# The first weight transfer of a decode kernel, as two transfers of 64 partitions

## The chip, the cores and the metric

The kernel runs on one core of a Trainium2 chip. A core has five engines that run side by side and meet only at semaphores: TensorE (PE; its weight loads are shown as PEld), VectorE (DVE), ScalarE (ACT), GpSimd (POOL) and SyncE (SP). Data is brought from the chip's memory (HBM) into the core's own memory of 128 partitions by sixteen DMA engines. In this kernel every transfer is issued by SP, whose instructions appear in the profile as SPq.

The metric is the device time of one execution in microseconds. The kernel before was run three times: 364.06, 364.42 and 364.50, median 364.42.

## The reference

The kernel computes one decode step for 8 sequences: a gated sum of attention over a window of a key/value cache and a small multilayer network.

```
x = A_x                                       # 8 x 1 x 576, bf16
g = sigmoid((x * gate_w).sum(-1))
q = (x @ wq)                                  # wq: 576 x 4096; 32 heads of 128
k, v = last W = 2048 rows of the caches       # 16 KV heads, each for two query heads
p = softmax(q . k * 128 ** -0.5)
a = (p @ v) @ wo                              # wo: 4096 x 576
h = gelu(layernorm(x) @ w1 + b1)              # w1: 576 x 4608
b = h @ w2 + b2                               # w2: 4608 x 576
out = g * a + (1 - g) * b
```

Each of the two caches contributes 8 sequences x 16 heads x 2048 rows x 128 values in bf16, 67 MB. With the weights some 154 MB have to be read for an output of 9 KB.

## The kernel before

All operations are first described to a planner (`_Plan`, lines 39 to 164), not issued. `add` describes one operation on one engine with its dependencies and an estimated cost; `dma` (line 56) describes a transfer with the issuing engine, a semaphore and a size. A transfer may also have `after`, other transfers that must be issued earlier on the queue without being waited for. `schedule` (line 62) goes through all operations by their estimated times and so fixes the order on every engine. It models one shared stream for transfers of at least 65,536 bytes and charges each issue 0.35 us of the engine's own time (lines 98 to 103). `emit` (line 141) then writes each engine's instructions in this order, with the semaphore waits that the dependencies need. A wait on a DMA semaphore is a wait for a count: each transfer adds 16 when it has landed, so an operation that needs two transfers on one semaphore waits for 32, one that needs three for 48.

The core's memory is one arena. Its largest part, `RAW`, has four slots of 32 KB in each partition and some room behind them. At the start the slots hold weights: the main part of the query matrix (rows 0 to 511, `wq_m`, 32 KB in each partition) lies in slot 0, `w1` in slot 3, and the last 64 rows of the query matrix (`wq_r`, lines 357 and 358) behind `w1`. These 64 rows of 4096 values are cut in two, so that they fill 128 partitions with 2048 values (4 KB) each: partition 2k has the first half of row 512 + k, partition 2k + 1 the second. `xT` is laid out to match: the matmuls over this part (`q_fn`, lines 506 to 515, t = 4) contract over all 128 partitions with weights of x that are zero in every other one.

Lines 407 to 418 describe the first transfers, all on SP and chained by `after` in this order: `d_wqr` (the last rows of the query matrix, 512 KB), `d_wqm` (its main part, 4096 KB), x (9 KB), the gate's weights, two biases, `d_w1m` and `d_w1r` (4608 and 576 KB). The list `dwq` holds the two query transfers; the query matmuls `q_pe` depend on both and on the transposed x.

Behind them SP issues the stream (lines 586 to 594): 16 transfers of K and 16 of V, 4096 KB each, alternating from the second K on (`load_item`, line 613, issue at line 618), then parts of `w2` (line 865) and `wo` (line 836), and at the end the output (line 903). The first two K go into slots 1 and 2, which are free from the start. Every later transfer waits on SP until its slot is free: K slots are freed by the DVE transposes (line 718), V slots by the matmuls with the softmax weights (lines 755 and 188), slot 0, for the first V, by `q_pe`, and slot 3, for the third K, by the matmuls over `w1`.

For each K item the DVE transposes the keys, PE computes the scores (line 732 and the held matmuls of line 175), DVE takes the maximum (line 645), ACT the exponential (line 649), and DVE and ACT spread the result (lines 668 and 674) for the matmuls with V. The query itself is made once, from 13.9 to 25 us: x is transposed, multiplied with the query weights, rearranged and copied (lines 422 to 537). At the very end the last three parts of `w2` are multiplied in (line 579), the sum is copied out (lines 900 and 901) and stored.

Of the kernel before, what the change touches and what calls it, by code (L numbers as in the profile page):

```python
# [38 lines left out]
class _Plan:  # L39
# [16 lines left out]
    def dma(self, eng, fn, semkey, nbytes, deps=(), name=None, after=(), prio=0):  # L56
        op = _Op(eng, fn, deps, name, self.DMA_ISSUE, after=after, is_dma=True, dma_sem=semkey, nbytes=nbytes, prio=prio)
        op.idx = len(self.all)
        self.all.append(op)
        return op  # L60
# [134 lines left out]
def build_kernel(nc, A_x, A_k_cache, A_v_cache, A_wq, A_wo, B_x, B_w1, B_b1, B_w2, B_b2, gate_w, out):  # L195
# [29 lines left out]
    with ExitStack() as es:  # L225
# [129 lines left out]
        wq_m = RAW[:, 0:4 * 4096].rearrange("p (t c) -> p t c", t=4)  # L355
        W1O = (ND - 1) * DE
        WQR = W1O + 4 * F + F // 2
        wq_r = RAW[:, WQR:WQR + 2048]
# [21 lines left out]
        add, dma = P.add, P.dma  # L380
# [23 lines left out]
        o_on8 = add("pool", lambda e: e.memset(ones8, 1.0), name="ones8", cost=0.15)  # L404


        d_wqr = dma("sp", lambda e: e.dma_start(wq_r, A_wq[512:576, :].rearrange("k (s c) -> (k s) c", s=2)), "wq", 64 * 8192, name="d_wqr")
        d_wqm = dma("sp", lambda e: e.dma_start(wq_m.rearrange("p t c -> p (t c)"), A_wq[0:512, :].rearrange("(p t) c -> p (t c)", t=4)), "wq", 512 * 8192, name="d_wqm", after=[d_wqr])
        dwq = [d_wqm, d_wqr]
        d_x = dma("sp", lambda e: e.dma_start(x_sb, x2), "x", 8 * D * 2, name="d_x", after=[d_wqm])  # L410
        d_gw = dma("sp", lambda e: e.dma_start(gw_sb, gate_w.partition_broadcast(1)), "g", D * 2, name="d_gw", after=[d_x])
        d_b1 = dma("sp", lambda e: e.dma_start(b1c, B_b1.rearrange("(c f) -> c f", c=FC)), "b", F * 2, name="d_b1", after=[d_gw])
# [500 lines left out]
def bass_gated_mix__sliding_block_cached__mixer_channel_mlp__decode_kernel(  # L913
    nc: bass.Bass,
    A_x: bass.AP,
    A_k_cache: bass.AP,
    A_v_cache: bass.AP,
    A_wq: bass.AP,
    A_wo: bass.AP,
    B_x: bass.AP,  # L920
    B_w1: bass.AP,
    B_b1: bass.AP,
    B_w2: bass.AP,
    B_b2: bass.AP,
    gate_w: bass.AP,
    out: bass.AP,
):
    build_kernel(nc, A_x, A_k_cache, A_v_cache, A_wq, A_wo, B_x, B_w1, B_b1, B_w2, B_b2, gate_w, out)
# [28 lines left out]
```

## Time and profile before

| | before |
|---|---|
| three runs, median | 364.42 us |
| the profiled execution's own time | 364.27 us |
| its span, first to last instruction | 363.0 us |
| mean granted TensorE clock | 0.958 |
| packets of the data queue | 6092, 154.30 MB |
| read from HBM over the span | 425 GB/s |
| first issue on SP | 0.80 us |
| first landing that an engine waits for (x) | 13.86 us |
| last issue on SP (the output) | 361.61 us |

The span is counted from the first instruction to the last; the profiled execution's own time has 1.3 us more around it. The profile's page lists each engine's busy time, then the span in 40 slices of 9.1 us: each digit is a tenth of a slice. The row "GB/s" is what the DMA engines moved in each slice. Its table of queues has the data transfers as q1; q8 and q14 fetch instructions. "The chain that ended last" goes back from the last instruction, at each step to what released it. Other views used below are the list of DMA issues (KB of each, median us from issue to landing), the chain in order of time (start, duration, what), the timeline of one engine (start, duration, engine, line, operation) and the view by windows: for stretches of the span the busy time and number of instructions of each engine, the granted clock, the DMA share and GB/s. In that last view a DMA packet is counted whole in the stretch in which it starts, so that the share of a short stretch can be over 1.

### The profile page before, as it was taken

Reading aid. Unit: us, or ns where it says so; the run is one execution under the profiler, and the core shown is the slowest. Engines: PE = TensorE matmul, PEld = TensorE weight load, DVE = VectorE, ACT = ScalarE, POOL = GpSimd, SP = SyncE. Lnnn points to the kernel's source line nnn. Section 1 sums busy time; section 2 is a strip of 40 time slices with the busy share of each in tenths; the row PEclk is TensorE's granted clock in tenths of the full one; section 3 lists DMA queues with packets and bytes.
Section 4 is the critical chain, followed back from the end, with each engine's and each line's share of the span. In section 5 each row is a group of like instructions: output and inputs, shape, how many; then the busy total and the mean of one; then the engine's idle time right before and its main releaser. Section 6 shows DMA issues by size and latency. Waiting matters only on the chain.

```text
span 363.0 us, 4821 instructions
## 1 busy us (share of the span) xinstructions
PE 297.9 (82%) x1954; PEld 125.3 (35%) x1423; DVE 231.4 (64%) x166; ACT 168.6 (46%) x130; POOL 22.9 (6%) x52
## 2 busy tenths in 40 slices
PE   0456366999999979998897979997989698999875
PEld 0111000434252615242433417150615152436742
DVE  0452989576666694929385768566675949295720
ACT  1022106656647463663637373838374554656000
POOL 9032030000010000000100000000000000003000
PEclk9976598999999998999999989999999999999999
DMA  8999999999999999999999999999999999999996
GB/s 347 436 437 406 455 412 455 412 455 412 450 415 451 415 451 413 441 426 441 426 441 426 435 430 437 430 437 428 437 430 437 430 435 430 437 430 433 415 430 257
DMA packets 6102, 154.45 MB, mean 426 GB/s; under 512 B 694, under 2 KB 840, under 8 KB 1228
## 3 DMA queue, kind: packets, MB, share of 16 engines
q1 hardware_dynamic: 6092, 154.30, 98.8%
q8 instruction: 8, 0.13, 0.1%
q14 instruction: 2, 0.02, 0.0%
HBM read 154.29 MB, written 0.01 MB: 425 GB/s over the span
## 4 chain that ended last, share of the span: by engine, by line
DMA 56%; DVE 27%; PE 14%; issue 1%; ACT 1%; SPq 0%; POOL 0%
DMA arena<-in_A_k_cache_dram 47%; DVE arena L718 21%; PE ps L175 6%; DMA arena<-in_B_w_dram 6%; DMA arena<-in_A_x_dram 3%; DVE arena L668 2%; PE ps L188 2%; PE ps L755 2%; PE ps L732 2%; DVE arena L645 1%; PE ps L501 0%; PE ps L579 0%; DVE arena L557 0%; DVE arena L521 0%; ACT arena L536 0%
## 5 line engine op out<-in xcount | busy, mean ns | idle before, releaser
L718 DVE STREAM_TRANSPOSE arena<-arena 128x4096 f32<-128x4096 f32 (+1 forms) x34 | 141.7, 4175 | 21.9 <-DMA arena<-in_A_k_cache_dram 21.9
L674 ACT ACTIVATE arena<-arena 32x2048 bf16<-32x2048 bf16 x60 | 114.5, 1908 | 71.4 <-DVE arena L668 42.9
L175 PE MATMUL ps<-arena 128*128 128x512 bf16 (+3 forms) x531 | 136.1, 402 | 0.0
L188 PE MATMUL ps<-arena 128*128 x840 | 109.5, 277 | 7.3 <-issue 1.2
L188 PEld LDWEIGHTS ps<-arena 128*128 x840 | 81.4, 97 | 34.3 <-issue 19.0
L732 PE MATMUL ps<-arena 128*128 128x512 bf16 x128 | 51.4, 401 | 27.6 <-DVE arena L718 26.1
L645 DVE TENSOR_REDUCE arena<-ps 128x1 f32<-128x2048 f32 x16 | 36.7, 2291 | 53.8 <-PE ps L175 53.8
L732 PEld LDWEIGHTS ps<-arena 128*128 128x128 bf16 x128 | 12.5, 98 | 131.7 <-issue 75.3
L649 ACT ACTIVATE arena<-ps,arena 128x2048 bf16<-128x2048 f32 x16 | 40.7, 2543 | 0.5
L646 ACT ACTIVATE arena<-arena 128x1 f32<-128x1 f32 x16 | 3.2, 203 | 63.5 <-DVE arena L645 63.5
L755 PE MATMUL ps<-arena 128*128 128x256 bf16 x184 | 25.3, 272 | 1.1 <-DVE arena L663 1.1
L755 PEld LDWEIGHTS ps<-arena 128*128 128x128 bf16 x184 | 16.9, 99 | 18.8 <-issue 14.6
L668 DVE STREAM_TRANSPOSE arena<-arena 128x1024 f32<-128x1024 f32 x15 | 18.1, 1205 | 2.9 <-ACT arena L649 2.9
L579 PE MATMUL ps<-arena 128*8 128x288 bf16 (+1 forms) x140 | 9.6, 286 | 4.0 <-DMA arena<-in_A_wo_dram 3.3
L739 POOL MEMSET arena<- 128x4096 f32 x1 | 3.5, 3511 | 148.2 <-PE ps L175 148.2
L685 PE MATMUL ps<-arena 128*128 128x512 bf16 x16 | 6.5, 407 | 6.5 <-ACT arena L649 5.2
L629 POOL COPY arena<-arena 32x64 bf16<-32x64 bf16 x16 | 3.7, 229 | 123.3 <-PE ps L175 122.4
L901 ACT ACTIVATE arena<-ps 8x288 bf16<-8x288 f32 x1 | 0.4, 402 | 19.5 <-PE ps L579 19.5
L422 DVE COPY arena<-arena 8x128 bf16<-8x128 bf16 x2 | 0.5, 228 | 13.9 <-DMA arena<-in_A_x_dram 13.9
L579 PEld LDWEIGHTS ps<-arena 128*8 128x8 bf16 (+1 forms) x140 | 5.8, 86 | 9.9 <-DMA arena<-in_A_wo_dram 3.3
L900 DVE CAST arena<-ps 8x288 bf16<-8x288 f32 x1 | 0.4, 446 | 12.3 <-PE ps L579 12.3
L557 DVE TENSOR_TENSOR arena<-arena 128x1152 f32<-128x1152 f32 x1 | 1.4, 1358 | 9.7 <-ACT arena L555 9.7
(106 smaller groups left out, 94.0 us busy)
## 6 DMA issues: line engine op xcount, KB each, us to landing
arena<-in_A_k_cache_dram SPq DMA_DIRECT2D x16, 4096.0 KB, 28.7
arena<-in_A_v_cache_dram SPq DMA_DIRECT2D x16, 4096.0 KB, 25.5
arena<-in_B_w_dram SPq DMA_DIRECT2D x1, 4608.0 KB, 22.0
arena<-in_A_wo_dram SPq DMA_DIRECT2D x2, 2304.0 KB, 23.8
arena<-in_A_wq_dram SPq DMA_DIRECT2D x1, 4096.0 KB, 12.6
arena<-in_B_w_dram SPq DMA_DIRECT2D x1, 3456.0 KB, 24.1
arena<-in_B_w_dram SPq DMA_DIRECT2D x1, 1152.0 KB, 22.3
arena<-in_B_w_dram SPq DMA_DIRECT2D x1, 576.0 KB, 23.0
```

Source lines behind the costliest of these rows:

```text
L175: return e.add_instruction(mybir.InstMatmult(name=nc.get_next_instruction_name(), engine=mybir.EngineType.PE, ins=[e.lower_ap(rhs), e.lowe ...
L188: return e.add_instruction(mybir.InstMatmult(name=nc.get_next_instruction_name(), engine=mybir.EngineType.PE, ins=[rhs, lhsT], outs=[e.low ...
L579: ins = e.matmul(ps[32 * j:32 * j + 8, BK_ACC, 0:JN], lhsT, rhs[:, JN * j:JN * j + JN], start=False, stop=True, skip_group_check=True, til ...
L629: return e.tensor_copy(dst, src)
L645: mx = add("dve", lambda e: e.tensor_reduce(out=k(g, MX + x), in_=scores, axis=AXL.X, op=ALU.max), deps=[qk_unit[t]], name="mx%d" % t, cos ...
L649: ex = add("act", lambda e: e.activation(out=bass.AP(arena, offset=aoffs("P"), ap=[[AST, 128], [64, 32], [1, 2], [2, 32]]), in_=ps[:, 0:4, ...
L668: pc = add("dve", lambda e: e.transpose(view("PC").bitcast(F32), view("P").bitcast(F32)), deps=[ex] + (sp_done[t - 1][0] if t else [o_acc0 ...
L674: return e.activation(out=bass.AP(arena, offset=32 * a * AST + aoffs(home) + 64 * a, ap=[[AST, 32], [256, 32], [1, 64]]), in_=bass.AP(aren ...
L685: mm = e.matmul(*args, start=True, stop=False, skip_group_check=True) if n == 0 else held_matmul(nc, e, *args, start=True, stop=False, ski ...
L718: return e.transpose(bass.AP(arena_f, offset=foffs(base) + 2048 * h0, ap=[[AST // 2, 128], [1, 2048 * nh]]), bass.AP(arena_f, offset=foffs ...
L732: mm = e.matmul(*args, start=False, stop=True, skip_group_check=True) if rc == 0 else held_matmul(nc, e, *args, stop=True, skip=True)
L755: return e.matmul(dst, bass.AP(arena, offset=aoffs(home) + 256 * q + ee, ap=[[AST, 128], [2, 128]]), slot(s).rearrange("p (r k d) -> p r k ...
```

## The change

The transfer `d_wqr` of 128 partitions is replaced by two, `d_wqr0` for partitions 0 to 63 and `d_wqr64` for partitions 64 to 127. They have the same source bytes, the same destination and the same semaphore, are chained one behind the other, and the main part comes behind the second. `dwq` now has three transfers. Nothing else is touched.

```diff
-        d_wqr = dma("sp", lambda e: e.dma_start(wq_r, A_wq[512:576, :].rearrange("k (s c) -> (k s) c", s=2)), "wq", 64 * 8192, name="d_wqr")
-        d_wqm = dma("sp", lambda e: e.dma_start(wq_m.rearrange("p t c -> p (t c)"), A_wq[0:512, :].rearrange("(p t) c -> p (t c)", t=4)), "wq", 512 * 8192, name="d_wqm", after=[d_wqr])
-        dwq = [d_wqm, d_wqr]
+        dwq = []
+        for p0 in (0, 64):
+            dwq.append(dma("sp", (lambda p0=p0: lambda e: e.dma_start(wq_r[p0:p0 + 64], A_wq[512:576, :].rearrange("k (s c) -> (k s) c", s=2)[p0:p0 + 64]))(),
+                           "wq", 32 * 8192, name="d_wqr%d" % p0, after=dwq[-1:]))
+        d_wqm = dma("sp", lambda e: e.dma_start(wq_m.rearrange("p t c -> p (t c)"), A_wq[0:512, :].rearrange("(p t) c -> p (t c)", t=4)), "wq", 512 * 8192, name="d_wqm", after=dwq[-1:])
+        dwq.append(d_wqm)
```

## The prediction

> **What bounds the kernel now.** I read the page first: its slices and its table of DMA queues.
>
> ```profile
> span 363.0 us, 4821 instructions
> PE 297.9 (82%) x1954; PEld 125.3 (35%) x1423; DVE 231.4 (64%) x166; ACT 168.6 (46%) x130; POOL 22.9 (6%) x52
> ...
> DMA  8999999999999999999999999999999999999996
> GB/s 347 436 437 406 455 412 455 412 455 412 450 415 451 415 451 413 441 426 441 426 441 426 435 430 437 430 437 428 437 430 437 430 435 430 437 430 433 415 430 257
> DMA packets 6102, 154.45 MB, mean 426 GB/s; under 512 B 694, under 2 KB 840, under 8 KB 1228
> ...
> q1 hardware_dynamic: 6092, 154.30, 98.8%
> q8 instruction: 8, 0.13, 0.1%
> ```
>
> The DMA engines are busy in every slice but the first and the last, and no compute engine is above 82%. The kernel is one stream of 154 MB: what it loses at its start it can get back only if it stands idle later. The view by windows, where a packet counts in the stretch in which it starts (columns: the engines, the granted clock, the DMA share, GB/s), shows that it does not stand idle:
>
> ```profile
> 60.00:100.00 40.00, 38.01 (x222) 14.51 (x152) 27.85 (x9) 26.32 (x18) 0.00 (x0) 1.00 1.00 432
> ...
> 180.00:220.00 40.00, 34.30 (x211) 14.08 (x149) 26.79 (x22) 20.62 (x15) 0.00 (x0) 0.96 1.00 433
> ...
> 260.00:300.00 40.00, 34.03 (x223) 15.03 (x160) 29.11 (x23) 21.32 (x16) 0.00 (x0) 1.00 1.00 432
> ```
>
> Share 1.00, and 432 GB/s whatever the cores compute. A transfer of K or V (4096 KB, 4.19 MB) takes 4.19 MB / 432 GB/s = 9.7 us of this stream, but lands 25 to 29 us after its issue (DMA issues, then pieces of the chain of waits in order of time):
>
> ```profile
> arena<-in_A_k_cache_dram SPq DMA_DIRECT2D x16, 4096.0 KB, 28.7
> arena<-in_A_v_cache_dram SPq DMA_DIRECT2D x16, 4096.0 KB, 25.5
> ...
> arena<-in_A_wq_dram SPq DMA_DIRECT2D x1, 512.0 KB, 3.3
> ...
> arena<-in_B_w_dram SPq DMA_DIRECT2D x1, 144.0 KB, 22.9
> ```
> ```profile
> 1.71 12.15 DMA arena<-in_A_x_dram
> ...
> 79.66 25.41 DMA arena<-in_A_k_cache_dram
> ...
> 337.03 22.31 DMA arena<-in_B_w_dram
> ...
> 359.38 1.71 PE ps L579 x24
> ...
> 361.12 0.45 DVE arena L900
> ```
>
> So about 25.4 - 9.7 = 15.7 us of earlier transfers stand ahead of each new one. An issue may come many microseconds later without emptying the queue; a byte that moves later moves the end. From the last landing to the end, 359.34 to 363.0, nothing changes.
>
> **The start, which the change touches.** The timeline of SP's queue:
>
> ```profile
> 0.80 0.39 SPq L407 DMA_DIRECT2D arena<-in_A_wq_dram  x1
> 1.25 0.41 SPq L408 DMA_DIRECT2D arena<-in_A_wq_dram  x1
> 1.71 0.37 SPq L410 DMA_DIRECT2D arena<-in_A_x_dram  x1
> ...
> 4.11 1.26 SPq L618 DMA_DIRECT2D arena<-in_A_k_cache_dram  x2
> 19.39 0.54 SPq L618 DMA_DIRECT2D arena<-in_A_v_cache_dram  x1
> ```
>
> and the windows of the first four microseconds, in quarters and halves:
>
> ```profile
> 1.50:1.75 0.25, 0.00 (x0) 0.00 (x0) 0.00 (x0) 0.25 (x1) 0.25 (x2) 1.00 0.00 0
> ...
> 3.25:3.50 0.25, 0.00 (x0) 0.00 (x0) 0.00 (x0) 0.00 (x0) 0.25 (x2) 1.00 3.13 1294
> 3.50:3.75 0.25, 0.00 (x0) 0.00 (x0) 0.00 (x0) 0.00 (x0) 0.25 (x3) 1.00 2.58 1081
> 3.75:4.00 0.25, 0.00 (x0) 0.00 (x0) 0.00 (x0) 0.00 (x0) 0.25 (x2) 1.00 0.00 0
> ```
> ```profile
> 1.75:2.25 0.50, 0.00 (x0) 0.00 (x0) 0.00 (x0) 0.33 (x1) 0.50 (x3) 1.00 0.57 131
> 2.25:2.75 0.50, 0.00 (x0) 0.00 (x0) 0.00 (x0) 0.00 (x0) 0.50 (x4) 1.00 1.02 385
> 2.75:3.25 0.50, 0.00 (x0) 0.00 (x0) 0.00 (x0) 0.00 (x0) 0.50 (x2) 1.00 0.96 393
> ```
>
> No byte starts before 1.75, so a transfer's first row starts about 1.0 us after its issue begins at 0.80. The first transfer is 128 rows of 4 KB. 131 GB/s x 0.5 us = 65 KB, 16 rows, start by 2.25; 385 x 0.5 = 192 KB, 47 more, by 2.75; 48 more by 3.25. In the two quarters after that 1294 x 0.25 = 323 KB and 1081 x 0.25 = 270 KB start: the big rows (32 KB) of the main transfer, some eight or nine in the first quarter and eight in the second. So the sixteen engines enter the main transfer within half a microsecond, in two groups roughly 0.25 us apart.
>
> **The change part by part.** *One more issue on SP.* L407's transfer is removed, two are put in its place, each with 64 rows: one instruction more on SP. The steps between issues are 0.45 (0.80 to 1.25) and 0.46, so the main transfer is issued at 1.70 instead of 1.25, x at 2.16, the first K at 4.56. What hides it: the main transfer's 4.19 MB, which x, the biases, w1 and K stand behind. The next issue after the first two of K, at 19.39, waits for a slot and not for SP. Nothing new waits on a semaphore: the query matmuls wait for three landings instead of two, the last of them the same main transfer. Could the stream run dry between the halves? With 1.0 us from issue to first row, half 2 is ready at 2.25 and the main transfer at 2.70. Even at today's rate the 63rd row starts only by 2.75, so half 1 lasts until then, and 111 rows have started by 3.25, so half 2 lasts beyond that: margins of 0.5 us each. Cost 0; with the cover gone, up to 0.45.
>
> *Two transfers that each cover half of the partitions.* The bytes are the same, 524,288, which at 432 GB/s take 1.21 us. What a wide load to 64 partitions runs at, this trace doesn't show. The nearest rows are the narrow ones: x, 8 rows of 1152 B into 8 partitions, which start in 13.10 to 13.20; the last rows of w2, of the same size (144 KB in 128 rows) but over 128 partitions; and the output, 8 such rows out of 8 partitions.
>
> ```profile
> 13.10:13.20 0.10, 0.00 (x0) 0.00 (x0) 0.00 (x0) 0.00 (x0) 0.00 (x0) 1.00 0.19 58
> ...
> 360.20:360.40 0.20, 0.20 (x6) 0.01 (x2) 0.00 (x0) 0.00 (x0) 0.00 (x0) 1.00 0.22 75
> ...
> 362.30:362.60 0.30, 0.00 (x0) 0.00 (x0) 0.00 (x0) 0.00 (x0) 0.00 (x0) 1.00 0.13 31
> ```
>
> GB/s over share is the rate of 16 busy engines: 75 / 0.22 = 341 over 128 partitions, 58 / 0.19 = 305 for x, 31 / 0.13 = 238 for the output. Rows that several engines move at one small set of partitions are slower in one case by 1.4 times and hardly in the other. That the partitions a transfer covers limit it is thus hinted at, not shown. Bounds: if the engines don't disturb each other, 0, or a small gain. If sixteen engines crowd into half of the way into the memory, the rate halves for as long as all work on the same half: 2.42 us instead of 1.21, +1.21. But the two groups are 0.25 us apart: at the end of each half the early group is already in the other half (or in the main transfer) and both run undisturbed. Two such stretches take off 2 x 0.25: +0.71. The middle of 0.71 and 1.21 is 0.96.
>
> [...]
>
> *An earlier start of the late engines.* In the first half microsecond 16 rows start where 432 x 0.5 = 216 KB would be 53: the ramp loses 37 rows, 152 KB, 0.35 us. If half as many rows to prepare let the second group start sooner, at most about half of it, 0.2, comes back; the other bound is 0. I take 0.1 off.
>
> *The planner.* It lays out all queues by estimated times. Both halves are over its bound of 65,536 bytes and together occupy its modelled stream as long as before, so I expect the same order everywhere: 0.
>
> Sum: 0 + 0.96 - 0.1 + 0 = 0.86, rounded +0.9. The profiled execution took 364.27; 364.27 + 0.9 = 365.17. The median of the runs shown, 364.42, is 0.15 above it: **365.3 us**.
>
> **The rivals.** *The halves cost nothing*: the engines take the rows of both halves back to back, as the x row (305 against 341) suggests. Not slower: 364.4. For it speaks that today's transfer is short, and that much of its time is ramp; against it the output's row.
>
> *The start gets better*: the 0.2 above without the crowding, 364.2. The full ramp back would be 364.42 - 0.35 = 364.1.
>
> *Another engine is last*. The end waits for the slowest of sixteen engines, and the eight instruction packets each hold one of them: 0.1% of 16 x 363 us is 5.8 us, 0.7 us each (by rounding 0.4 to 1.1). If the packet that now delays the last engine falls on one that is ahead, the end comes up to 0.7 earlier: 363.7; a little more with the ramp's gain, 363.5. It decides once the engines' order among each other changes by more than the 0.25 us between the groups. Against it: the fetches follow the compute engines' programs, which don't change.
>
> *A hole in the stream*: if half 2 or the main transfer needs 0.5 us longer to its first row than the first does, the margins are gone and the stream stops for up to 0.45: 364.9.
>
> **How the numbers follow.** Crowding, my forecast, 0.60; no cost 0.20; the better start 0.06; another engine last 0.08; a hole 0.06. A measurement of this kernel can tell about 0.2%, 0.73 us, from no change: slower begins at 365.15, faster at 363.69. The forecast's own range is +0.6 to +1.3, 365.0 to 365.7; 0.53 of its 0.60 lies above 365.15 and 0.07 below. Slower is 0.53 and 0.02 of the hole: 0.55. Faster is 0.07 of another engine last and 0.01 of the better start: 0.08. The rest, 0.37, is the same. The range reaches from the full ramp's gain, 364.1, to 1.21 with part of a hole (0.25) on top, 365.9; outside are the other engine (0.07), some of the better start, and about 0.06 above.
>
> **What would show it.** In the changed profile: three issues of query weights 0.45 apart, and no stretch between 2.0 and 4.5 us with share near 0 before the main transfer's rows start (no hole). Crowding shows as share near 1 at about half the GB/s between 2.25 and 4.25, the big rows starting about 0.9 later than 3.25 to 3.75, x landing about 0.9 later than now (1.71 + 12.15 = 13.86), and equal distances after that: 432 GB/s throughout and the last landing near 360.2. I am wrong in the mechanism if GB/s over share stays near today's 390 in these stretches, and wrong in the carry if the start is later but the end is not.

## The result and the profile after

The changed kernel takes 365.90 us (median of 8 runs, 365.22 to 367.11) against 364.50 us (8 runs, 364.06 to 364.87) of the kernel before on the same chip: 1.4 us slower by the medians. The ratio, here and in the tables below, is estimated from all runs and so differs a little from that of the medians; here it is 1.0043 with an interval of 1.0028 to 1.0058. A second series of the same code, below, gave +2.7 us. The forecast was 365.3, +0.9, with 365.0 to 365.7 as its own range: the sign was right, the size was not.

The page of the changed kernel (the profiled execution took 366.86 us; its span is 365.3):

```profile
span 365.3 us, 4803 instructions
...
DMA  8999999999999999999999999999999999999996
GB/s 287 381 408 453 431 449 413 456 409 452 424 436 427 434 434 425 449 413 452 413 449 423 440 423 441 431 431 447 413 449 420 445 418 445 423 441 428 416 436 249
```

The two rows differ from before at their left edge: 287, 381 and 408 GB/s in the first three slices, where before has 347, 436 and 437. The rest is one stream as before. The view by windows (busy time of the engines, granted clock, DMA share, GB/s) and three pieces of the chain of waits in order of time (start, duration, what) say the same:

```profile
40.00:300.00 260.00, 225.26 (x1343) 91.72 (x960) 184.41 (x106) 138.78 (x100) 5.35 (x9) 0.96 1.00 432
```
```profile
2.67 13.99 DMA arena<-in_A_x_dram
...
339.57 22.05 DMA arena<-in_B_w_dram
...
361.66 1.74 PE ps L582 x24
```

x lands at 2.67 + 13.99 = 16.66 (before 13.86), the last weights at 339.57 + 22.05 = 361.62 (before 359.34): of the 2.8 us that this execution has lost by 16.7 us, 2.3 are still missing at the end, and between 40 and 300 us nothing is won or lost. All of this execution's difference arises at the start. The timeline of SP's queue and the windows there:

```profile
0.80 1.20 SPq L409 DMA_DIRECT2D arena<-in_A_wq_dram  x2
2.05 0.58 SPq L411 DMA_DIRECT2D arena<-in_A_wq_dram  x1
2.67 0.38 SPq L413 DMA_DIRECT2D arena<-in_A_x_dram  x1
```
```profile
1.75:2.25 0.50, 0.00 (x0) 0.00 (x0) 0.00 (x0) 0.33 (x1) 0.50 (x3) 1.00 0.61 66
2.25:2.75 0.50, 0.00 (x0) 0.00 (x0) 0.00 (x0) 0.00 (x0) 0.50 (x4) 1.00 0.53 74
2.75:3.25 0.50, 0.00 (x0) 0.00 (x0) 0.00 (x0) 0.00 (x0) 0.50 (x2) 1.00 1.05 410
3.25:3.75 0.50, 0.00 (x0) 0.00 (x0) 0.00 (x0) 0.00 (x0) 0.50 (x3) 1.00 1.05 254
3.75:4.25 0.50, 0.00 (x0) 0.00 (x0) 0.00 (x0) 0.00 (x0) 0.50 (x2) 1.00 1.23 303
4.25:4.75 0.50, 0.00 (x0) 0.00 (x0) 0.00 (x0) 0.00 (x0) 0.50 (x1) 1.00 1.80 598
```

Three things are to be seen. The two halves occupy SP for 1.20 us, 0.6 each and not 0.45, so the main transfer is issued at 2.05 and not at 1.70. Between 2.25 and 2.75 only 74 GB/s start, where before started 385: the ramp is slower. And between 3.25 and 4.25 the engines are busy for 254 / 1.05 = 242 and 303 / 1.23 = 246 GB/s, against 410 / 1.05 = 390 just ahead and 390 before the change: that is what the prediction named as the sign of crowding. The big rows begin in the last line, 1.0 us later than before.

### The profile page after: what moved, and what is told of

It is laid out like the page before. It is cut to its first block, busy times and chain, and to the rows that moved or that the text cites. A ratio compares the mean times of both kernels' runs of the same rounds, so it can differ in the third digit from the quotient of the medians.

```text
span 365.3 us, 4803 instructions
## 1 busy us (share of the span) xinstructions
PE 295.2 (81%) x1935; PEld 125.2 (34%) x1423; DVE 231.4 (63%) x166; ACT 168.6 (46%) x130; POOL 23.0 (6%) x52
## 4 chain that ended last, share of the span: by engine, by line
DMA 49%; PE 25%; DVE 22%; issue 2%; ACT 1%; SPq 0%; POOL 0%
DMA arena<-in_A_k_cache_dram 39%; DVE arena L721 16%; PE ps L175 11%; PE ps L188 6%; DMA arena<-in_B_w_dram 6%; DMA arena<-in_A_x_dram 4%; PE ps L735 3%; PE ps L758 2%; DVE arena L671 2%; DVE arena L648 1%; PE ps L582 0%; PE ps L504 0%; DVE arena L560 0%; DVE arena L524 0%; PE ps L688 0%
## 5 line engine op out<-in xcount | busy, mean ns | idle before, releaser
L735 PE MATMUL ps<-arena 128*128 128x512 bf16 x122 | 48.9, 400 | 18.9 <-DVE arena L721 17.2
L425 DVE COPY arena<-arena 8x128 bf16<-8x128 bf16 x2 | 0.5, 228 | 16.7 <-DMA arena<-in_A_x_dram 16.7
L688 PE MATMUL ps<-arena 128*128 128x512 bf16 x11 | 4.4, 399 | 5.2 <-ACT arena L652 5.2
```

Of the source, the lines that this page charges most:

```text
L688: mm = e.matmul(*args, start=True, stop=False, skip_group_check=True) if n == 0 else held_matmul(nc, e, *args, start=True, stop=False, ski ...
L735: mm = e.matmul(*args, start=False, stop=True, skip_group_check=True) if rc == 0 else held_matmul(nc, e, *args, stop=True, skip=True)
```

## The experiments

The kernels of each series ran on one chip, beside the kernel before (364.52 to 364.62; differences below are against its median in the same series). The first theory was the prediction's: P, crowding of the 64 partitions. Against it stood at first N, that the number or the form of the transfers costs, and later T, that the third transfer in the queue comes late, and L, that a transfer needs a minimum time between its issue and its turn.

### Series 1: is it the 64 neighbouring partitions?

The changed kernel again (e1), then its halves made of even and odd partitions (e2) and of columns over all 128 partitions (e3), and a K transfer in two halves, in the full stream, with the first transfer whole as before (e4). Edits of e2 and e3 against the changed kernel, of e4 against the kernel before:

```diff
-            dwq.append(dma("sp", (lambda p0=p0: lambda e: e.dma_start(wq_r[p0:p0 + 64], A_wq[512:576, :].rearrange("k (s c) -> (k s) c", s=2)[p0:p0 + 64]))(),
+            dwq.append(dma("sp", (lambda s0=s0: lambda e: e.dma_start(wq_r[s0:128:2], A_wq[512:576, 2048 * s0:2048 * s0 + 2048]))(),
```
```diff
+            dwq.append(dma("sp", (lambda c0=c0: lambda e: e.dma_start(wq_r[:, c0:c0 + 1024], A_wq[512:576, :].rearrange("k (s c) -> (k s) c", s=2)[:, c0:c0 + 1024]))(),
```
```diff
+            if nm == "dk" and t == 1:
+                for h in range(2):
+                    d = dma("sp", (lambda h=h: lambda e: e.dma_start(slot(s)[64 * h:64 * h + 64], src[16 * h:16 * h + 16]))(), "s%d" % s, 4 * W * Dh * 2, deps=slot_free[s], name="%s%d_%d" % (nm, t, h), after=last_dma[-1:])
```

> The changed kernel once more, for its spread and a second profile. In its first profile the main query transfer (4.19 MB, 128 partitions, itself unchanged) ran slower than before (x landed at 16.66 instead of 13.86, +2.8, of which only about 1 us is explained by the rows of the two halves starting later). Theory M: that slower main transfer is an accident of how the sixteen engines stand to each other, and comes in some executions only: then this profile can have x landing near 15.5 and a time of 365.5, or near 16.7 and a time near 366.8. Rival: it always follows from the split: x near 16.7 in every profile. Ratio to before 1.003 to 1.006 under both.

> Two transfers of 64 rows of 4 KB as in the change, but the first fills the 64 even partitions and the second the 64 odd ones, so that each reaches over the whole memory. Theory P (64 neighbouring partitions are written at half the rate): no crowding, 0 to +0.4 us, ratio 1.000 to 1.001, x landing at 13.9 to 14.3. Rival N (one more transfer, with fewer rows each, issued more slowly and started later): as the change, +1.0 to +1.6 us, ratio 1.003 to 1.005.

> Two transfers of all 128 partitions with half of the columns each (128 rows of 2 KB). Theory P: each reaches all partitions, 0 to +0.4 us, ratio 1.000 to 1.001. Rival N: one transfer more, +0.5 to +1.6 us, ratio 1.001 to 1.005.

> The kernel before, with the query matrix whole; instead the second K transfer (4.19 MB, in the midst of the stream) is split into two of 64 neighbouring partitions with rows of 32 KB. Theory P: its two halves run at half the rate, 19.4 us instead of 9.7 less some overlap: +8 to +9.7 us, ratio 1.022 to 1.027, and a stretch of the stream with full DMA share at about 216 GB/s. Rival N: one issue more behind a full queue: 0 to +0.3 us, ratio 1.000 to 1.001, 432 GB/s throughout.

| | median us (range) | against before, 364.58 | ratio, interval |
|---|---|---|---|
| e1, the change again | 367.28 (365.33 to 368.32) | +2.70 | 1.0066 [1.0042, 1.0090] |
| e2, even and odd partitions | 367.25 (365.82 to 367.65) | +2.67 | 1.0065 [1.0049, 1.0080] |
| e3, columns | 366.80 (366.16 to 367.13) | +2.22 | 1.0060 [1.0047, 1.0073] |
| e4, K in halves | 374.86 (374.64 to 375.10) | +10.28 | 1.0282 [1.0267, 1.0296] |

e4 shows the crowding at full size. One 4.19 MB transfer takes 9.7 us of the stream; at half rate it would take 9.7 more, and 10.3 were measured (the 0.6 on top is not assigned to anything). The windows of 20 us around it, first of before, then of e4:

```profile
35.00:55.00 20.00, 9.37 (x32) 0.87 (x8) 18.28 (x9) 2.70 (x4) 3.51 (x1) 0.74 1.02 441
```
```profile
35.00:55.00 20.00, 9.02 (x31) 0.88 (x8) 17.25 (x8) 1.96 (x2) 3.51 (x1) 1.00 1.03 223
...
60.00:70.00 10.00, 7.37 (x27) 0.73 (x7) 7.65 (x3) 6.57 (x4) 0.00 (x0) 0.75 0.99 429
```

Share 1.03 in one and 1.02 in the other, but 223 GB/s instead of 441, and back at 429 afterwards: the engines are not idle, they are slow. Why 64 neighbouring partitions take half the rate, no run shows.

But e2 and e3 tell against P as the whole: halves that cover partitions from one end to the other cost as much as the change. Something else at the start costs 2 us and more.

They also show that busy but slow engines are no sign of 64 neighbours by themselves. In the two microseconds from 3.25, first of before, then of e3:

```profile
3.25:5.25 2.00, 0.00 (x0) 0.00 (x0) 0.00 (x0) 0.00 (x0) 2.00 (x6) 1.00 1.33 559
```
```profile
3.25:5.25 2.00, 0.00 (x0) 0.00 (x0) 0.00 (x0) 0.00 (x0) 2.00 (x6) 1.00 1.31 372
```

559 / 1.33 = 420 GB/s and 372 / 1.31 = 284, though each half of e3 covers all 128 partitions. So the 242 and 246 GB/s of the changed profile do not prove crowding by themselves; that 64 neighbours crowd is shown by e4 above and by e10 against e17 below.

e1 fits neither of its expectations. Its profiled execution took 367.41, and yet x lands early in it: the first copy of x, which waits for that landing, starts at 15.18, only 1.3 later than before (13.89). The rest shows at the end. The last microsecond before the last weights land (at 359.34 and at 362.24), first of before, then of e1:

```profile
358.34:359.34 1.00, 0.43 (x8) 0.09 (x2) 0.00 (x0) 0.00 (x0) 0.00 (x0) 1.00 0.80 318
```
```profile
361.24:362.24 1.00, 0.47 (x8) 0.12 (x4) 0.00 (x0) 0.00 (x0) 0.00 (x0) 1.00 0.07 30
```

A share of 0.07 is about one engine of sixteen: the others have finished, and the end waits for the last one. So the landing of x does not tell the end, and two executions of the same code can lose their time in different ways.

### Series 2: which part of the start?

e5 splits another early transfer, the last rows of w1 (590 KB), which stands in the full stream, and leaves the query transfers as they were. e6 splits nothing and only puts x (9 KB) ahead of the main transfer. e7 is the change with the last rows of w1, whole, between the halves and the main transfer. e8 has the main transfer first and the last 64 rows, whole, behind it.

```diff
+            d_w1r = dma("sp", (lambda p0=p0: lambda e: e.dma_start(w1_r[p0:p0 + 64], B_w1[512:576, :].rearrange("k (s c) -> (k s) c", s=2)[p0:p0 + 64]))(),
```
```diff
+        d_x = dma("sp", lambda e: e.dma_start(x_sb, x2), "x", 8 * D * 2, name="d_x", after=[d_wqr])
+        d_wqm = dma("sp", lambda e: e.dma_start(wq_m.rearrange("p t c -> p (t c)"), A_wq[0:512, :].rearrange("(p t) c -> p (t c)", t=4)), "wq", 512 * 8192, name="d_wqm", after=[d_x])
```
```diff
+        d_w1r = dma("sp", lambda e: e.dma_start(w1_r, B_w1[512:576, :].rearrange("k (s c) -> (k s) c", s=2)), "w1", 64 * F * 2, name="d_w1r", after=dwq[-1:])
...
-        last_dma = [d_w1r]
+        last_dma = [d_w1m]
```
```diff
+        d_wqr = dma("sp", lambda e: e.dma_start(wq_r, A_wq[512:576, :].rearrange("k (s c) -> (k s) c", s=2)), "wq", 64 * 8192, name="d_wqr", after=[d_wqm])
```

> The query matrix whole as before; the last rows of w1 (576 KB, 128 rows of 4.6 KB, in the full stream behind 9 MB) as two transfers of 64 neighbouring partitions. Nothing happens at the start. Theory P alone (half the partitions, half the rate): 590 KB at 216 instead of 432 GB/s is +1.37 us, less overlap of the engines: +0.7 to +1.4 us, ratio 1.002 to 1.004. Rival: what costs is the start of the stream alone: +0.0 to +0.2, ratio 1.000 to 1.0005. If the mere number of transfers at the start were the cost, the main query transfer here would be disturbed too (x landing after 14.5).

> The query matrix's last rows whole, but the small transfer of x (9 KB) goes between them and the main part: the main part is issued about 0.45 us later behind the same 512 KB, and the order of the rest stays. Theory N1 (the main transfer's rows are not ready on all engines when the short first transfer is used up, because it is issued later): its first rows come late on some engines, +0.5 to +2 us, ratio 1.0015 to 1.006. Rival N2 (the two transfers of half the size are what disturbs, by their form): 0 to +0.2 us, ratio 1.000 to 1.0005.

> The change's two halves, then the last rows of w1 (576 KB, whole) ahead of the main query transfer: the main transfer is issued still later (about 2.6) but behind 1.1 MB instead of 0.5. N1 (late rows of the main transfer for want of cover): the main transfer starts on all engines without a gap; what is left is the crowding of the halves and their later first row: +0.8 to +1.3 us, ratio 1.002 to 1.0035. Rival N2 (the form of the halves disturbs whatever follows): as the change or worse, +1.4 to +2.7 us, ratio 1.004 to 1.0075.

> The main query transfer is issued first, at 0.80, its last rows whole behind it. It shows when the sixteen engines get the first rows of a big transfer with nothing in front. N1: the engines get them spread over 1 us or more and slowly, so that the stream starts worse than before: +0.5 to +2 us, ratio 1.0015 to 1.006. Rival: a big transfer is ready as fast as a small one, 0 to -0.2 us, ratio 0.9995 to 1.000.

| | median us (range) | against before, 364.62 | ratio, interval |
|---|---|---|---|
| e5, w1's last rows in halves | 365.64 (365.39 to 365.82) | +1.02 | 1.0028 [1.0017, 1.0039] |
| e6, x ahead of the main transfer | 366.49 (365.78 to 367.19) | +1.87 | 1.0053 [1.0040, 1.0066] |
| e7, a cover behind the halves | 366.62 (365.54 to 366.90) | +2.00 | 1.0047 [1.0035, 1.0059] |
| e8, main transfer first | 364.85 (364.64 to 365.16) | +0.23 | 1.0007 [0.9998, 1.0016] |

e5 is the crowding alone: +1.02 for 590 KB, which take 590 / 432 = 1.37 us of the stream; less than a doubling, as the prediction argued, though the interval, 0.6 to 1.4 us, just reaches one. e6 speaks against N: no transfer is split, and yet it loses 1.9 us. At the start it has the 9 KB of x ahead of the main transfer, which is issued at 1.66 instead of 1.25 (the planner also orders some later work of DVE and GpSimd otherwise, and no run has that alone):

```profile
1.25 0.36 SPq L408 DMA_DIRECT2D arena<-in_A_x_dram  x1
1.66 0.34 SPq L409 DMA_DIRECT2D arena<-in_A_wq_dram  x1
```

e7 costs more than the +0.8 to +1.3 that a cover should leave. A likely reason is that the transfer that stands third, now w1's rows, is issued at 2.05 in place of the main one; no run shows it. e8 misses its first expectation, +0.5 to +2, too: a large transfer at the head of the queue costs no more than 0.2.

### Series 3: the moment of the main transfer's issue

e9 is the kernel before with the main transfer held back on SP by one dependency, 0.50 us. e10 has the main transfer first and the two halves of 64 behind it, in the full stream. e11 issues the main transfer from ACT at the same time as SP issues the first one. e12 is the change with the second half issued from ACT.

```diff
+        d_wqm = dma("sp", lambda e: e.dma_start(wq_m.rearrange("p t c -> p (t c)"), A_wq[0:512, :].rearrange("(p t) c -> p (t c)", t=4)), "wq", 512 * 8192, name="d_wqm", deps=[o_ident], after=[d_wqr])
```
```diff
+        dwq = [d_wqm]
+        for p0 in (0, 64):
+            dwq.append(dma("sp", (lambda p0=p0: lambda e: e.dma_start(wq_r[p0:p0 + 64], A_wq[512:576, :].rearrange("k (s c) -> (k s) c", s=2)[p0:p0 + 64]))(),
```
```diff
+        d_wqm = dma("act", lambda e: e.dma_start(wq_m.rearrange("p t c -> p (t c)"), A_wq[0:512, :].rearrange("(p t) c -> p (t c)", t=4)), "wq", 512 * 8192, name="d_wqm", after=[])
```
```diff
+            dwq.append(dma("act" if p0 else "sp", (lambda p0=p0: lambda e: e.dma_start(wq_r[p0:p0 + 64], A_wq[512:576, :].rearrange("k (s c) -> (k s) c", s=2)[p0:p0 + 64]))(),
```

> The order of before (last rows whole, then the main query transfer as the second), but SP holds the main transfer until GpSimd has made its identity matrix, which before ended at 1.73: it is issued at about 1.8 instead of 1.25, behind the same 512 KB. Theory L (a big transfer that is issued once data is flowing gets its rows late on some engines; the first transfer is too short a cover): +1 to +2.5 us, ratio 1.003 to 1.007, some engines' first main rows after 4.0. Rival T (it is the third transfer of the queue that is late, whenever it is issued; here the third is x, behind 4 MB): +0 to +0.3 us, ratio 1.000 to 1.001.

> The main query transfer first, then the two halves of 64 partitions as in the change, behind 4 MB. The whole last rows in this place took 364.85 (e8_mainfirst). Crowding alone, as the w1 halves showed it (+1.02 for 590 KB): +0.9 for 524 KB, so 365.6 to 365.9, ratio to before 1.0027 to 1.0037. If the cost of the change lies in the start alone: 364.8 to 365.0, ratio 1.0005 to 1.001.

> Last rows whole on SP's queue, the main query transfer issued by ACT at the same time. Both are issued at 0.8. Theory L and theory T: no late rows; the same as before, 364.2 to 364.8, ratio 0.999 to 1.0005; perhaps up to 0.3 us faster, since SP is free 0.45 us earlier and the ramp has more rows to choose from.

> The change with its second half issued by ACT instead of SP, beside the first. Each engine has rows of both halves at hand, and the main transfer is the second on SP's queue. If the extra transfer ahead of the main one in SP's queue is the cost (L and T): 364.6 to 365.4, ratio 1.000 to 1.002. If any transfer of 64 partitions at the start costs what the change does: 365.8 to 367.3, ratio 1.0035 to 1.0075.

| | median us (range) | against before, 364.55 | ratio, interval |
|---|---|---|---|
| e9, main transfer 0.5 us later | 366.91 (366.38 to 367.89) | +2.36 | 1.0068 [1.0054, 1.0083] |
| e10, main first, then halves | 365.99 (365.67 to 366.20) | +1.44 | 1.0040 [1.0027, 1.0053] |
| e11, main from ACT | 365.01 (364.94 to 365.25) | +0.46 | 1.0014 [1.0005, 1.0023] |
| e12, second half from ACT | 366.46 (365.33 to 367.20) | +1.91 | 1.0056 [1.0044, 1.0068] |

e9 is the clearest run of the study: the main transfer issued 0.50 us later, and with it what stands behind it on SP, nothing else, and the end 2.4 us later. It also lets T fall, since the main transfer is the second here. e11 costs 0.5, more than expected, and is not explained. e12 lies 1 us above its first expectation and inside the second; what can be said of it stands below.

### Series 4: the same moment with more in front, and a smaller delay

e15 holds the main transfer back by 0.10 us only (issued at 1.35). e13 puts w1's last rows, whole, between the first transfer and the main one, which is then issued at 1.71 as in e9, but with 1.1 MB ahead of it instead of 0.5. e14 is e13 with the main transfer held back to 2.63. e16 has w1's last rows first, then the two halves, then the main transfer.

```diff
+        d_wqm = dma("sp", lambda e: e.dma_start(wq_m.rearrange("p t c -> p (t c)"), A_wq[0:512, :].rearrange("(p t) c -> p (t c)", t=4)), "wq", 512 * 8192, name="d_wqm", deps=[o_ones], after=[d_wqr])
```
```diff
+        d_w1r = dma("sp", lambda e: e.dma_start(w1_r, B_w1[512:576, :].rearrange("k (s c) -> (k s) c", s=2)), "w1", 64 * F * 2, name="d_w1r", after=[d_wqr])
+        d_wqm = dma("sp", lambda e: e.dma_start(wq_m.rearrange("p t c -> p (t c)"), A_wq[0:512, :].rearrange("(p t) c -> p (t c)", t=4)), "wq", 512 * 8192, name="d_wqm", after=[d_w1r])
```

e14 is the same with `deps=[o_r8]`; e16: `d_w1r` first, then the changed kernel's loop over the halves.

> Last rows of the query matrix (512 KB, whole), last rows of w1 (576 KB, whole), then the main query transfer, issued at about 1.71 as the third, behind 1.1 MB: its rows are needed some 3.3 us after its issue instead of 1.8 to 2. Theory L (lead: rows of a transfer issued while data flows reach some engines only 3 to 4 us after its issue): no or hardly any late rows, 364.4 to 365.2, ratio 0.9995 to 1.002. Rival (any big transfer that is issued third, or late, disturbs the stream whatever stands in front): 366 to 367, ratio 1.004 to 1.007.

> As e13, but SP holds the main transfer until GpSimd has made the r8 table (2.60 before): issued at about 2.65 behind the same 1.1 MB, so needed about 2.4 us after its issue. Theory L: late rows come back, 365.5 to 367, ratio 1.0025 to 1.007, engines idle around 5 us. Rival: 1.1 MB are cover enough, as e13.

> As e9, but held only until the memset of the ones, which before ended at 1.32: the main transfer is issued at about 1.37 instead of 1.25, 0.12 later, against 0.50 in e9 (+2.36). If each bit of lead counts: +0.3 to +1.0 us, ratio 1.001 to 1.003. If there is a step, between 1.25 and 1.37 (data starts to flow at 1.8): +1.5 to +2.5. If the step is later: 0 to +0.2.

> The change's two halves behind the last rows of w1 (576 KB, whole, issued first), the main query transfer behind them, issued at about 2.4 and needed some 3 us later. Theory L with crowding: the lead is enough, crowding alone is left: +1.0 to +1.3 us, ratio 1.0027 to 1.0037, in a narrow spread. Rival (the halves disturb what is behind them in some other way): +1.4 to +2.7 us in a wide spread, as the change in its two series.

| | median us (range) | against before, 364.60 | ratio, interval |
|---|---|---|---|
| e13, 1.1 MB ahead, issue at 1.71 | 364.87 (364.38 to 365.28) | +0.27 | 1.0007 [0.9998, 1.0016] |
| e14, 1.1 MB ahead, issue at 2.63 | 364.81 (364.43 to 365.32) | +0.21 | 1.0009 [0.9999, 1.0018] |
| e15, 0.5 MB ahead, issue at 1.35 | 364.57 (364.17 to 365.10) | 0.0 | 1.0000 [0.9991, 1.0009] |
| e16, w1's rows, halves, main | 365.85 (365.38 to 366.04) | +1.25 | 1.0033 [1.0021, 1.0046] |

e9 and e15 are one kernel with two delays. Their issues and windows, first e15, then e9:

```profile
1.35 0.33 SPq L408 DMA_DIRECT2D arena<-in_A_wq_dram  x1
```
```profile
1.75:3.75 2.00, 0.00 (x0) 0.00 (x0) 0.00 (x0) 0.33 (x1) 2.00 (x9) 1.00 1.41 524
3.75:5.75 2.00, 0.00 (x0) 0.00 (x0) 0.00 (x0) 0.00 (x0) 2.00 (x4) 1.00 0.63 262
...
3.75:9.75 6.00, 0.45 (x1) 0.13 (x1) 0.00 (x0) 0.00 (x0) 6.00 (x7) 1.00 0.96 410
9.75:19.75 10.00, 4.67 (x48) 1.11 (x28) 4.62 (x12) 0.80 (x3) 0.78 (x2) 1.00 0.97 418
```
```profile
1.75 0.33 SPq L408 DMA_DIRECT2D arena<-in_A_wq_dram  x1
```
```profile
1.75:3.75 2.00, 0.00 (x0) 0.00 (x0) 0.00 (x0) 0.33 (x1) 2.00 (x9) 1.00 0.96 393
3.75:5.75 2.00, 0.00 (x0) 0.00 (x0) 0.00 (x0) 0.00 (x0) 2.00 (x4) 1.00 0.57 197
...
3.75:9.75 6.00, 0.45 (x1) 0.13 (x1) 0.00 (x0) 0.00 (x0) 6.00 (x7) 1.00 0.90 322
9.75:19.75 10.00, 3.83 (x36) 0.93 (x24) 3.89 (x11) 0.59 (x3) 0.23 (x1) 1.00 0.98 423
```

By 9.75 us, e15 has started 2 x 524 + 6 x 410 = 3508 KB and e9 2 x 393 + 6 x 322 = 2718 KB: 790 KB less, at 432 GB/s 1.8 us. (A packet counts whole where it starts, and a packet of 32 KB on each of sixteen engines is 0.5 MB, so this is a rough figure.) In the ten microseconds after that both run alike, 418 and 423. Where e9 loses it, the first two rows show when taken together, since a single short row is blurred by the big packets: in the four microseconds from 1.75 the packets of e15 fill 2 x 1.41 + 2 x 0.63 = 4.1 us of the engines' time, those of e9 only 2 x 0.96 + 2 x 0.57 = 3.1. The main transfer is issued as this stretch begins and stands next, and still a quarter of the engines' time passes idle. The packets in progress, counted in the two traces at each tenth of a microsecond, say the same: e15 has 16 or more from 2.3 us on; e9 has 15 or more from 2.5 to 3.5, 8 or 9 from 3.6 to 4.6, and 16 again only from 6.4.

Idle engines are not the whole loss. The two microseconds from 5.25, first of e15, then of e9:

```profile
5.25:7.25 2.00, 0.45 (x1) 0.13 (x1) 0.00 (x0) 0.00 (x0) 2.00 (x2) 1.00 0.95 410
```
```profile
5.25:7.25 2.00, 0.45 (x1) 0.13 (x1) 0.00 (x0) 0.00 (x0) 2.00 (x2) 1.00 0.97 262
```

The packets fill the same share and carry a third less, as in e3, because rows last longer: of the rows of 32 KB that start before 7.5 us, the longest takes 1.45 us in e15 and 2.43 in e9. Why they do, no run shows. The end waits for the slowest engine, as in e1, so it loses more than the mean.

With 1.1 MB ahead, issues at 1.71 and 2.63 cost at most 0.3 us; for the second, e14, L had expected 0.9 to 2.4. e13 has no such gap; its packets fill 2 x 0.90 + 2 x 1.24 = 4.3 us of the same four:

```profile
1.75:3.75 2.00, 0.00 (x0) 0.00 (x0) 0.00 (x0) 0.33 (x1) 2.00 (x9) 1.00 0.90 306
3.75:5.75 2.00, 0.00 (x0) 0.00 (x0) 0.00 (x0) 0.00 (x0) 2.00 (x4) 1.00 1.24 513
```

e16 against e13 has the halves as its main difference, and they cost 365.85 - 364.87 = 0.98.

### Series 5: the crowding alone, and the last theory of lateness

e17 is e10 with even and odd partitions in place of neighbours. e18 is e13 with the main transfer held back to 3.57, so that it has no more time between its issue and its turn than in e9. An estimate of that time: the first row moves at 1.8, the ramp loses 0.35, 1.1 MB take 2.6 at 432 GB/s, so the turn comes near 4.7 and the issue 1.2 ahead of it; in e9, with 0.5 MB (1.2 us), it comes near 3.4, 1.6 after the issue.

```diff
+            dwq.append(dma("sp", (lambda s0=s0: lambda e: e.dma_start(wq_r[s0:128:2], A_wq[512:576, 2048 * s0:2048 * s0 + 2048]))(),
```
```diff
+        d_wqm = dma("sp", lambda e: e.dma_start(wq_m.rearrange("p t c -> p (t c)"), A_wq[0:512, :].rearrange("(p t) c -> p (t c)", t=4)), "wq", 512 * 8192, name="d_wqm", deps=[o_sel], after=[d_w1r])
```

> As e10 (main query transfer first, two transfers of 64 rows behind its 4 MB), but the first takes the even partitions and the second the odd ones. Everything is the same as in e10 but which partitions a transfer covers. Crowding of 64 neighbours is the cost in e10 (365.99): then here nothing but the order is left, 364.7 to 365.1, ratio 1.0003 to 1.0015. If it is the form of 64 rows or the one transfer more: 365.7 to 366.2 again, ratio 1.003 to 1.0045.

> As e14, but SP holds the main transfer until GpSimd has made the table sel (3.53 before): issued at about 3.55 behind the same 1.1 MB, so its rows are needed 1.3 to 1.7 us after the issue (e14: 2.3 to 2.6, no late rows, 364.81). Theory L, with the bound that the runs so far give (2.0 to 2.3 us of lead are enough, 1.6 to 2.0 are not): late rows, +1 to +3 us, ratio 1.003 to 1.008. Rival: the early time of issue or a first transfer of only 512 KB was what mattered, and behind 1.1 MB nothing happens: 364.6 to 365.2, ratio 1.000 to 1.0015.

| | median us (range) | against before, 364.52 | ratio, interval |
|---|---|---|---|
| e17, main first, then even and odd | 364.99 (364.83 to 365.17) | +0.47 | 1.0012 [1.0003, 1.0021] |
| e18, 1.1 MB ahead, issue at 3.57 | 365.00 (364.66 to 365.18) | +0.48 | 1.0013 [1.0004, 1.0022] |

e10 and e17 differ in nothing but which partitions a half covers, and with them which part of the rows: +1.44 and +0.47, so neighbours cost 1.0 us for 524 KB. The number and the form of the transfers, N, are the same in both, and e17 is 0.24 above e8, which has one transfer there. One row of each shows it, the first copy of x, which stands behind the halves in the queue (e10, then e17):

```profile
15.70 0.23 DVE L424 COPY arena<-arena 8x128 bf16<-8x128 bf16 x1 [15.70 <-DMA arena<-in_A_x_dram]
```
```profile
14.57 0.23 DVE L424 COPY arena<-arena 8x128 bf16<-8x128 bf16 x1 [14.57 <-DMA arena<-in_A_x_dram]
```

x lands 1.13 us earlier in e17.

e18 lets L fall: by the estimate above its main transfer has less time than e9's, and it costs 0.5 where e9 costs 2.4.

**What stands of the lateness, and what is open.** The main transfer issued at 1.25 (before) and at 1.35 (e15, 0.0) was on time. Issued between 1.66 and 2.05, which is about when the first rows begin to move (between 1.75 and 2.25 in before and in the change), and behind only 0.5 MB, it was late, and the kernels took 1.4 to 2.7 us more (e2, e3, e6, e9 and the change; e2 and the change at 2.04 and 2.05); the packets counted in e9 and in the change show it late on some of the engines. Behind 1.1 MB it cost 0.2 to 0.5, whether issued at 1.71, 2.63 or 3.57. (e12, with half a transfer ahead on its own queue and half on another, issues the main one at 1.43 and loses 1.9; as it crowds too, it says little here.) Two readings fit all of these: that issues in this moment are slow, and 1.1 MB hide it at 1.71; or that the bytes queued ahead decide. An issue at 2.6 behind 0.5 MB would help to tell them apart and was not run. That it costs 2 us where the delay is 0.5 is seen in e9 as idle engines and longer rows, and in e1 as a last engine that ends alone; what makes them so is open.

No version is faster than the kernel before; e15, which is the kernel before but for 0.1 us, is level with it.

## Why the prediction was wrong

**The bound, right.** The stream sets the time, what is lost at the start is carried to the end, and nothing gives it back: 432 GB/s from 40 to 300 us as before, and the last landing 2.3 us later in a span that is 2.3 longer.

**The step that failed: "Could the stream run dry between the halves? [...] margins of 0.5 us each. Cost 0; with the cover gone, up to 0.45."** It took 0.45 us for each issue and 1.0 us from issue to first row from the transfers of before, and held that for the main transfer too. Neither holds. A transfer of 64 rows keeps SP 0.6 us, so the main one is issued at 2.05 and not at 1.70. And its rows are not there on all engines 1.0 us later: e9 shows the cost of a late issue without any split, +2.36, and e2 and e3 show it with splits that do not crowd, +2.7 and +2.2. The price of the rival "a hole in the stream", 364.9, had a part of the mechanism, engines without rows, and was about a fifth of what e9 measured. The half microseconds of the changed profile have no share near 0, which the prediction had named as the sign that there is no hole; that sign was too weak, since a part of the engines was busy while others waited: counted in the changed trace, 9 to 15 packets are in progress from 4.3 to 5.0 us, and 16 or more from 2.5 to 4.2.

**The crowding, right.** Forecast +0.96 between 0.71 and 1.21; measured 1.0 (e10 against e17) and 0.98 (e16 against e13) for the same 524 KB, and 1.02 (e5) for 590 KB. That the middle of two far bounds fits so closely is in part luck: by their intervals these three are known to about 0.6, 0.6 and 0.4 us. That they are less than a doubling, 1.21 and 1.37, is what all three say, but each interval reaches the doubling, so it is not shown. In e4, with 4.19 MB, where changes between halves hardly count, it is the full doubling, 10.3 us for 9.7.

**The earlier start of the late engines, wrong sign.** Instead of -0.1, the first half microsecond from 2.25 on starts 74 GB/s in place of 385: (385 - 74) x 0.5 = 156 KB, or 0.36 us at 432 GB/s. No run separates this loss from the others.

**The planner, right.** The order of the engines' work is unchanged.

**The rivals.** "The halves cost nothing" and "the start gets better" fell with the first result. "Another engine is last" named the right thing, that the slowest engine sets the end, on the wrong side: that engine was later.

**The sum.** 1.4 and 2.7 us in the two series, with crowding at about 1.0. The rest, 0.4 to 1.7, is put down to the late main transfer and the slower ramp by subtraction; no execution of the change shows it by itself. In the first profile the engines without rows from 4.3 to 5.0 us make only about 0.2 us in the mean, and a part of the loss arises after 8 us, in the stretch described at the end, whose cause is open. In the second one engine ends alone. The two costs need not add up: crowded halves last longer and may so hide a part of the lateness, which would explain why e2, without crowding, is no cheaper than the change (between 1.75 and 7.0 us an engine stands idle for 1.3 us in the mean in e2's trace, for 0.7 in the change's).

## What to carry to other kernels

Split a transfer by partitions only so that each part still reaches the whole range of partitions: 64 neighbours halved the stream's rate (e4, 223 GB/s instead of 441), 64 of one parity in the full stream cost a quarter of a microsecond over one whole transfer (e17 against e8). In a kernel that is one stream of transfers, treat the first two microseconds as part of it: what SP issues ahead of the first large transfer was paid several times over where it pushed that issue to the moment when data begins to move with only 0.5 MB ahead (e9, 2.36 us for 0.50); with 1.1 MB ahead it cost 0.2 to 0.5 us. Price a new issue by its own shape, not by its neighbour's.

## What was not expected of the hardware

An issue 0.50 us later cost 2.36 us at the end (e9), one 0.10 us later nothing (e15). A transfer of 64 rows keeps SP longer than one of 128: 1.17 to 1.20 for two in the change, e2, e10, e16 and e17, 0.86 for two of 128 rows and half the width in e3, 0.39 for the first transfer of before; and the one behind such a pair takes 0.58 (the main transfer of the change) where e3's takes 0.42. The kernels with a late main transfer scatter: their medians stand in ranges of 1.0 (e3) to 3.0 us (e1), those of the others without a late one in 0.3 to 0.9.

In the change's first profile the sixteen engines were busy all the time from 8.4 to 13.9 us and moved less than before; the windows, first of the change, then of before:

```profile
8.40:13.90 5.50, 0.00 (x0) 0.00 (x0) 0.00 (x0) 0.00 (x0) 1.58 (x2) 1.00 1.00 387
```
```profile
8.40:13.90 5.50, 0.00 (x0) 0.00 (x0) 0.01 (x1) 0.00 (x0) 1.57 (x2) 1.00 1.06 451
```

387 / 1.00 against 451 / 1.06 = 425 GB/s. The second profile of the change (e1) has 393 / 0.91 = 432 there:

```profile
8.40:13.90 5.50, 0.00 (x0) 0.00 (x0) 0.00 (x0) 0.00 (x0) 1.58 (x2) 1.00 0.91 393
```

So it is not a property of the change; its cause is open.
